# An attention-plus-MLP kernel's boot: two products moved to GpSimd, small state copies to ScalarE, and fewer filler matmuls

## The chip, the cores and the metric

The kernel runs on one core of a Trainium2 chip. A core has five engines with queues of their own: TensorE (PE, with its weight loads as PEld), VectorE (DVE), ScalarE (ACT), GpSimd (POOL) and SyncE (SP, which here only issues DMAs). Each engine works through its instructions in order and waits on semaphores for the others. The metric is the device time of one execution in microseconds, as the median of several runs; the kernel before takes 544.73 us (three runs, 544.55 to 544.80).

## The reference: what is computed

A linear attention with a decaying state, whose output feeds a layer pair with an unusual activation. For each batch (4), head (8) and token (768), with head dimension 48:

```
y_t   = r_t (state + (u * k_t) v_t^T)
state = diag(w_t) state + k_t v_t^T
```

The outputs, as x of 3072 tokens by 384, go through h = x w_in (384 by 2048), g = h - tanh(h), and out = g w_out (2048 by 384). All is float32.

## The kernel before, in words

The 3072 tokens are cut into eight blocks of 384 (four batches, two halves of the sequence each). For each block the attention is computed in chunks of 64 tokens; its result, transposed, lies in three tiles xT0 to xT2, and the layer pair takes it in 16 steps f: `first` (L869) multiplies w_in by xT into PSUM, three products per f, and the second product follows some steps later. While the layer pair of one block runs, the attention of the next is prepared by operations that `plan` (L1053) puts at given steps f. The order of PE, DVE, ACT and SP is written out by hand: what stands first in the program is issued first. POOL's order is the program's too. Waits are added by the framework from the tiles that are read and written. The first layer product of step f is followed by some no-operation instructions on PE (`SPACED`, L80: three behind each product in the first steps of block 0), and in block 0 each second-layer product by one.

Before block 0 can begin, `boot` (L1128) does the attention of block 0 with nothing beside it. It works in two halves of four heads each: h1 (pairs 2 and 3) and h2 (pairs 0 and 1), `HALVES`. For a half it does the following.

- `behind` (L420): a scan from the right over the decays w on DVE, into `post`; `take_whole` (L447) takes the whole chunk's decay from it.
- `times_behind` (L439): post becomes k times the scan, 128x768 on DVE.
- `times_u` (L451): ACT scales k by u in place, two instructions.
- `before` (L413): a reciprocal and a scan from the left into `pre` on DVE. `times_before` (L433): pre becomes r times that scan, on DVE.
- `own` (L507) and `earlier` (L510): the products of each chunk, r with k and pre with post, on PE; what they return is the masked copy into the score tile A on DVE (L502). `gram` (L474) does the products, and can put filler matmuls ahead of them: `passed` (L308, tiny 16x16 ones; the argument spare, 94 in h1) and `busy` (L301).
- `turn_1`, `turn_2` (L513, L521): PE transposes post, ACT copies the result to ks. `totals_by_column` (L620): ACT lays out the decays for the scan over states.
- `update_half` (L602): PE multiplies ks with v into two PSUM tiles, hp and acc (`by_column`), for the half's two pairs. `states_half` (L626): DVE scans over them, one scan a pair, into `first_states`, and returns two small adds (L632) which form the state that goes to block 1.
- `result("from_states")`, `result("from_scores")`: PE multiplies first_states by pre and v by A into PSUM; with apart=True the first goes pair by pair (`from_states`, L663), without it the pairs take turns within each chunk. `result_out` (L720) copies to xT and to the tile `late`; ACT does one half and, for h2, DVE the other.
- `fill_holes` (L773): six small DMAs of `late` into rows of xT that the copies leave free, in turn from SP and POOL.

Weights come as raw 64-bit pieces by DMA from SP (`more_weights`, `load_weights` L248) into five buffers and are converted by ACT (three instructions) and DVE (one), `convert` (L253). `begin_behind` holds a load until a given matmul is done: here until the state products of h1, the own products of h2 and the earlier products of h2.

Of the kernel before, what the change touches and what calls it, by code (L numbers as in the profile page):

```python
# [46 lines left out]
ALU = mybir.AluOpType  # L47
# [3 lines left out]
B, H, S, D = 4, 8, 768, 48  # L51
P = 128
L = 64
NB = 384
NQ = S // NB
NCH = NB // L
# [5 lines left out]
UP = 2  # L62
HALVES = (UP, 0)
ALL = tuple(range(NPAIR))
# [3 lines left out]
KC = DM // P  # L68
# [10 lines left out]
LATE = 3  # L79
SPACED = (3, 0), (0, 3), (3, 2), (2, 3), (3, 2), (2, 3), (3, 0), (0, 0)  # L80

# [45 lines left out]
def kernel(  # L127
# [12 lines left out]
    nc = tc.nc  # L140
# [179 lines left out]
    class Block:  # L320
# [111 lines left out]

        def times_before(self, p0, n):  # L433

            t = self.before_each(p0, n)
            return nc.vector.tensor_tensor(out=t, in0=self.tokens("r", p0, n).rearrange("d (c t) -> d c t", t=L),
                                           in1=t, op=ALU.mult)

        def times_behind(self, p0, n):  # L439


            t = self.half("post", p0, n * NCH * LP + 2)[:, 2:].rearrange("d (c j) -> d c j", j=LP)[:, :, 0:L]
            return nc.vector.tensor_tensor(
                out=self.half("post", p0, n * NB).rearrange("d (c t) -> d c t", t=L),
                in0=self.tokens("k", p0, n).rearrange("d (c t) -> d c t", t=L), in1=t, op=ALU.mult)
# [61 lines left out]
        def own(self, ps, p0, **fill):  # L507
            return self.masked(ps, "k", "r", masks["diagonal"], p0, **fill)

        def earlier(self, ps, p0, **fill):  # L510
            return self.masked(ps, "post", "pre", masks["above"], p0, **fill)
# [114 lines left out]
        def states_half(self, p0):  # L626

            for p in reversed(range(UP)):
                to, by, kv = (t.rearrange("d e c -> d (e c)") for t in
                              (first_states[:, p0 + p], first_totals[:, p0 + p], self.by_column[p]))  # L630
                nc.vector.tensor_tensor_scan(out=to, data0=kv, data1=by, initial=0.0, op0=ALU.add, op1=ALU.mult)
            return [lambda p=p0 + p, kv=kv: nc.vector.tensor_tensor(  # L632
                out=states[1][:, p, 0, 0:D], in0=first_states[:, p, :, NCH - 1], in1=kv[:, :, 0], op=ALU.add)
                for p, kv in enumerate(self.by_column)]

# [96 lines left out]
        def together(self, ps):  # L732
# [34 lines left out]
            for of in (from_state, scores) if self.q else (scores, from_state):  # L767
                for cross in range(2):
                    stretch(of, cross)
            self.result_out(ALL)  # L770
            self.fill_holes([nc.sync])

        def fill_holes(self, engines, which=range(2 * KC)):  # L773
            for n in reversed(which):
                i, h = n // 2, n % 2
                src = 64 * (n // KC) + 16 * (n % KC)
                engines[n % len(engines)].dma_start(out=self.xT[i][64 * h + D:64 * h + 64],
                                                    in_=self.late[src:src + 16, :])

# [273 lines left out]
    def plan(i):  # L1053
# [3 lines left out]
        if i == 0:  # L1057
            phases = {6: ("turn",), 7: ("update",), 10: ("earlier",), 13: ("results",)}
            before = {0: ("behind 2", "take_whole 2"), 2: ("behind 0", "take_whole 0"), 3: ("times_behind 2",),
                      4: ("times_behind 0",), 5: ("before 2",), 6: ("before 0",), 7: ("times_before",),  # L1060
# [51 lines left out]
    def run(ops):  # L1112
        for op in ops:
            op()
# [13 lines left out]
    def boot(ps, pair, blk, later):  # L1128
# [11 lines left out]
        blk.behind(h1, 1)  # L1140
        blk.take_whole(h1, UP)
        blk.totals_by_column(h1)
        nc.scalar.copy(out=later_ident, in_=ident)
        blk.before(h1, UP)
        blk.times_behind(h1, UP)
        blk.times_u(h1, UP)
        own = blk.own(ps, h1, spare=94, ahead=5, late=6)
        blk.turn_1(ps, h1)
        blk.times_before(h1, UP)
        earlier = blk.earlier(ps, h1)  # L1150
        blk.behind(h2, UP)
        blk.take_whole(h2, UP)
        first_a, first_b = convert(*raws.pop(0), tiles=2)
        own()
# [3 lines left out]
        begin_behind(blk.done, more_weights(nc.sync))  # L1158
        blk.times_behind(h2, UP)
        blk.times_u(h2, UP)  # L1160
        blk.turn_1(ps, h2)
        blk.turn_2(h2)
        earlier()
        blk.results(ps)
        blk.result("from_scores", both[0])
        run(blk.states_half(h1))
        blk.result("from_states", both[0], True, apart=True)
        blk.before(h2, UP)
        blk.update_half(pair, h2)
        blk.times_before(h2, UP)  # L1170
        own = blk.own(ps, h2)
# [5 lines left out]
        scored = blk.done  # L1177
        onwards = blk.states_half(h2)
        own()
        run(first_a[1:])  # L1180
        needed = 2 * KC - 2
        blk.fill_holes([nc.sync, nc.gpsimd], range(needed, 2 * KC))
        begin_behind(own_scored, more_weights(nc.sync))
        blk.fill_holes([nc.sync, nc.gpsimd], range(needed))
        begin_behind(scored, more_weights(nc.sync))
# [6 lines left out]
        blk.yp.reverse()  # L1192
        blk.result("from_states", both[1], apart=True)
        earlier(1, 1)
# [4 lines left out]
        more_weights(nc.sync)  # L1199
        run(onwards)  # L1200
        run(first_b[:1])
# [251 lines left out]
```

## Time and profile before

| | us |
|---|---|
| median of three runs | 544.73 |
| the profiled execution | 545.07 |
| its span in the profile | 543.3 |
| PE busy in the span | 534.1 |
| DVE busy | 459.0 |
| ACT busy | 403.7 |
| POOL busy | 6.5 |
| end of the boot: first layer product (L871) begins | 23.50 |

A row of a timeline reads: start in the span, length, engine, line, operation, the tile written and the tile read with their sizes, and the count of merged instructions; in brackets the idle time before it and what ended that. The lengths of merged rows run from the first start to the last end, and neighbours overlap a little since engines are pipelined; the distance of two starts is the better price of an instruction. In the costliest groups a row has count, busy time, mean ns, and then the idle time before them. A matmul of float32 shows as two passes, so a layer step is six rows of PE.

### The profile page before, as it was taken

How to read it: one execution, taken by the hardware profiler on the slowest of the kernel's cores; microseconds unless marked ns; L12 is line 12 of the kernel's file. 1: busy time of each engine (PE TensorE's matmuls, PEld its weight loads, DVE VectorE, ACT ScalarE, POOL GpSimd, SP SyncE). 2: the span in 40 equal slices, each digit the busy share in tenths (PEclk: the TensorE clock that was granted, in tenths of full speed). 3: DMA queues.
4: the chain of work that ended last, by engine and by line, in shares of the span. 5: the costliest groups of instructions: out<-in, count | busy, mean ns of one | idle time of the engine just before them, and what ended most of it. 6: DMA issues, size and time to landing. Idle time of an engine off the chain costs nothing.

```text
span 543.3 us, 14866 instructions
## 1 busy us (share of the span) xinstructions
PE 534.1 (98%) x5682; PEld 403.3 (74%) x5682; DVE 459.0 (84%) x943; ACT 403.7 (74%) x814; POOL 6.5 (1%) x47
## 2 busy tenths in 40 slices
PE   7999999999999999999999999999999999999996
PEld 5756665678877777777887787877788788777874
DVE  7999999999989989798997979879797997557463
ACT  4899986888668876688767886688866885766561
POOL 1100000000000000000000000000000000000000
PEclk9999999999999999999999999999999999999999
DMA  7798732252311631154112532136321420100101
GB/s 276 234 402 311 259 119 74 97 137 63 122 42 54 162 118 57 43 147 119 60 56 87 122 103 70 48 97 151 84 89 46 122 27 3 56 1 0 45 1 46
DMA packets 53048, 56.34 MB, mean 104 GB/s; under 512 B 21488, under 2 KB 50928, under 8 KB 52976
## 3 DMA queue, kind: packets, MB, share of 16 engines
q1 hardware_dynamic: 52592, 55.18, 33.9%
q8 instruction: 48, 0.79, 0.6%
q14 instruction: 24, 0.20, 0.1%
q10 hardware_dynamic: 288, 0.10, 0.1%
q0 software_dynamic: 96, 0.07, 0.1%
HBM read 44.73 MB, written 4.72 MB: 91 GB/s over the span
## 4 chain that ended last, share of the span: by engine, by line
PE 88%; DVE 6%; ACT 2%; issue 2%; DMA 1%; SPq 0%; DVEq 0%
PE hp L871 41%; PE acc L999 27%; PE att L999 7%; PE att L757 4%; PE acc L950 3%; PE acc L977 2%; PE att L494 2%; PE att L575 1%; PE att L871 1%; ACT up L264 1%; DMA r<-in_rT 1%; DVE w_sb L268 1%; PE acc L871 1%; DVE scores L502 1%; DVE states L587 1%
## 5 line engine op out<-in xcount | busy, mean ns | idle before, releaser
L871 PE MATMUL hp<-xT,w_sb 128*128 128x384 f32 x738 | 259.3, 488 | 0.4 <-ACT h L876 0.4
L871 PEld LDWEIGHTS hp<-xT,w_sb 128*128 128x128 f32 x738 | 131.8, 190 | 70.0 <-ACT h L876 1.3
L999 PE MATMUL acc<-forms,g 128*128 128x128 f32 x954 | 133.2, 276 | 0.0
L876 ACT ACTIVATE h<-hp 128x384 f32<-128x384 f32 x123 | 60.3, 490 | 96.6 <-PE hp L871 96.5
L999 PEld LDWEIGHTS acc<-forms,g 128*128 128x128 f32 x954 | 122.0, 192 | 10.3
L879 DVE SCALAR_TENSOR_TENSOR h<-h,s 128x384 f32<-128x384 f32 x128 | 70.5, 551 | 51.9 <-ACT s L894 51.8
L920 DVE TENSOR_TENSOR g<-g 128x256 f32<-128x256 f32 x265 | 103.2, 418 | 7.4 <-PE acc L999 6.5
L895 ACT ACTIVATE qa<-s,shift 128x384 f32<-128x384 f32 x113 | 69.5, 615 | 3.7
L897 ACT ACTIVATE junk<-s,shift 128x384 bf16<-128x384 f32 x113 | 67.7, 599 | 0.0
L879 DVE SCALAR_TENSOR_TENSOR g<-qa,h 128x384 f32<-128x384 f32 x112 | 61.6, 550 | 1.6 <-ACT qa L905 0.2
L894 ACT ACTIVATE s<-h 128x384 f32<-128x384 f32 x113 | 59.2, 523 | 3.6
L999 PEld LDWEIGHTS acc<-w_sb,g 128*128 128x128 f32 x318 | 46.8, 191 | 9.7 <-ACT sums L967 0.3
L999 PE MATMUL acc<-w_sb,g 128*128 128x128 f32 x318 | 53.0, 276 | 0.0
L999 PE MATMUL att<-w_sb,g 128*128 128x128 f32 x212 | 35.5, 275 | 0.0
L999 PEld LDWEIGHTS att<-w_sb,g 128*128 128x128 f32 x212 | 31.1, 192 | 5.3
L1034 DVE TENSOR_TENSOR sums<-sums 128x256 f32<-128x256 f32 x84 | 32.8, 406 | 1.7 <-ACT sums L1011 1.4
L950 PE MATMUL acc<-w_sb,sums 128*128 128x384 f32 x96 | 33.9, 489 | 0.1
L264 ACT ACTIVATE up<-raw 128x768 f16<-128x768 f32 (+1 forms) x32 | 33.1, 1074 | 0.0
L950 PEld LDWEIGHTS acc<-w_sb,sums 128*128 128x128 f32 x96 | 17.9, 190 | 13.0 <-DVE sums L879 1.2
L417 DVE TENSOR_TENSOR_SCAN pre<-w,start 128x780 f32<-128x780 f32 x14 | 25.0, 1783 | 0.8
L429 DVE TENSOR_TENSOR_SCAN post<-w,seed 128x780 f32<-128x780 f32 x14 | 24.9, 1775 | 0.0
L897 ACT ACTIVATION_READ_ACCUMULATOR junk<-s,shift 128x1 f32 x113 | 21.1, 187 | 0.0
(118 smaller groups left out, 528.8 us busy)
## 6 DMA issues: line engine op xcount, KB each, us to landing
raw<-in_weights SPq DMA_DIRECT2D x16, 768.0 KB, 7.1
w<-in_wT SPq DMA_DIRECT2D x7, 780.0 KB, 4.7
k<-in_kT SPq DMA_DIRECT2D x7, 768.0 KB, 4.6
r<-in_rT SPq DMA_DIRECT2D x7, 768.0 KB, 4.6
v_sb<-in_v SPq DMA_DIRECT2D x8, 576.0 KB, 4.0
k<-in_tokens SPq DMA_DIRECT2D x7, 576.0 KB, 5.0
r<-in_tokens SPq DMA_DIRECT2D x7, 576.0 KB, 4.7
out_y<-sums SPq DMA_DIRECT2D x18, 128.0 KB, 1.8
```

The lines of the kernel that those rows point to most:

```text
L264: return lambda: nc.scalar.activation(out=to, in_=of, func=AF.Copy, scale=scale, bias=bias)
L417: return nc.vector.tensor_tensor_scan(out=self.tile("pre")[:, cols], data0=self.tile("w")[:, cols], data1=start[:, 0:n * NCH * LP], initia ...
L871: nc.tensor.matmul(hp, lhsT=w_in_sb[:, f, kc, :], rhs=xT[kc], start=(kc == KC - 1), stop=(kc == 0))
L876: return h, nc.scalar.activation(out=h, in_=hp, func=AF.Copy, scale=1.0 / UPSCALE)
L879: return lambda: nc.vector.scalar_tensor_tensor(out=out, in0=in0, scalar=scalar, in1=in1, op0=op0, op1=ALU.mult)
L894: nc.scalar.activation(out=s, in_=h, func=AF.Square)
L895: nc.scalar.activation(out=qa, in_=s, func=AF.Square, bias=shift[:, 4:5])
L897: nc.scalar.activation(out=junk[:, 0:NB], in_=s, func=AF.Relu, bias=shift[:, 5:6], accum_out=excess[:, at:at + 1])
L920: return lambda: nc.vector.tensor_tensor(out=G[:, to:to + 2], in0=two(G, g_at(q, a0), g_at(q, a1)), in1=two(G, g_at(q, b0), g_at(q, b1)), ...
L950: nc.tensor.matmul(acc, lhsT=g[:, j * P:(j + 1) * P], rhs=w_out_sb[:, f, :], start=(f == self.first), stop=(f == NF - 1))
L999: nc.tensor.matmul(to, lhsT=G[:, g_at(q, a), :], rhs=rhs, start=start, stop=stop, skip_group_check=True)
L1034: ops.append(lambda op=op, at=at: nc.vector.tensor_tensor(out=at[0], in0=at[1], in1=at[2], op=OPS[op]))
```

## The change

In `boot`: `times_behind` of h1 is issued before `totals_by_column` and `before`. `times_behind` and `times_before` of h2 are issued on POOL instead of DVE, the first right behind `take_whole`, the second behind `before` of h2. The four small adds that finish the state (L632) are split: ACT copies the last term of the sum from PSUM (`last_half`, two copies of 128x48 a half), and one add of 128x192 (`onwards`) follows in step 3 of block 0. For h1 the two copies stand between ACT's scaling by u for h2 and its copy to ks; for h2 between the first and the second weight piece. The masked copy of own products of h2 now comes before the scans over states of h2 on DVE. The products from states of h2 no longer go pair by pair. Four of the fills of holes go out on SP, and xT0's two on POOL. The tiny filler pairs are 38 instead of 94, and the no-operations behind the first layer's products of block 0 are six instead of three. In the kernel's general path, which this input does not take, result_out gets other copies.

```diff
@@ -77,7 +77,8 @@
 UNITS = [(0, 0), (0, 1)] + [u for j in range(NF // 2 - 2) for u in ((1, j), (0, j + 2))] + [(1, NF // 2 - 2),
                                                                                       (1, NF // 2 - 1)]
 LATE = 3
-SPACED = (3, 0), (0, 3), (3, 2), (2, 3), (3, 2), (2, 3), (3, 0), (0, 0)
+SPARE = 38
+SPACED = (6, 0), (0, 3), (3, 2), (2, 3), (3, 2), (2, 3), (3, 0), (0, 0)
 
 
 
@@ -430,17 +431,17 @@
                 out=back(t[:, 0:width]), data0=back(self.tile("w")[:, a:a + width]),
                 data1=back(seed[:, 0:width]), initial=1.0, op0=ALU.mult, op1=ALU.max)
 
-        def times_before(self, p0, n):
+        def times_before(self, p0, n, engine=nc.vector):
 
             t = self.before_each(p0, n)
-            return nc.vector.tensor_tensor(out=t, in0=self.tokens("r", p0, n).rearrange("d (c t) -> d c t", t=L),
+            return engine.tensor_tensor(out=t, in0=self.tokens("r", p0, n).rearrange("d (c t) -> d c t", t=L),
                                            in1=t, op=ALU.mult)
 
-        def times_behind(self, p0, n):
+        def times_behind(self, p0, n, engine=nc.vector):
 
 
             t = self.half("post", p0, n * NCH * LP + 2)[:, 2:].rearrange("d (c j) -> d c j", j=LP)[:, :, 0:L]
-            return nc.vector.tensor_tensor(
+            return engine.tensor_tensor(
                 out=self.half("post", p0, n * NB).rearrange("d (c t) -> d c t", t=L),
                 in0=self.tokens("k", p0, n).rearrange("d (c t) -> d c t", t=L), in1=t, op=ALU.mult)
 
@@ -629,9 +630,15 @@
                 to, by, kv = (t.rearrange("d e c -> d (e c)") for t in
                               (first_states[:, p0 + p], first_totals[:, p0 + p], self.by_column[p]))
                 nc.vector.tensor_tensor_scan(out=to, data0=kv, data1=by, initial=0.0, op0=ALU.add, op1=ALU.mult)
-            return [lambda p=p0 + p, kv=kv: nc.vector.tensor_tensor(
-                out=states[1][:, p, 0, 0:D], in0=first_states[:, p, :, NCH - 1], in1=kv[:, :, 0], op=ALU.add)
-                for p, kv in enumerate(self.by_column)]
+
+        def last_half(self, p0):
+
+            for p, kv in enumerate(self.by_column):
+                nc.scalar.copy(out=states[1][:, p0 + p, 0, 0:D], in_=kv[:, :, 0])
+
+        def onwards(self, p0, n):
+            to = states[1][:, p0:p0 + n, 0, 0:D]
+            nc.vector.tensor_tensor(out=to, in0=first_states[:, p0:p0 + n, :, NCH - 1], in1=to, op=ALU.add)
 
         def update_any(self, ps, p0, tot):
             ks, last = self.ks[:, p0:p0 + UP], self.q == NQ - 1
@@ -767,15 +774,14 @@
             for of in (from_state, scores) if self.q else (scores, from_state):
                 for cross in range(2):
                     stretch(of, cross)
-            self.result_out(ALL)
-            self.fill_holes([nc.sync])
-
-        def fill_holes(self, engines, which=range(2 * KC)):
+            self.result_out(ALL, None if spread else [nc.scalar.copy] * 2)
+            self.fill_holes()
+
+        def fill_holes(self, which=range(2 * KC), engine=nc.sync):
             for n in reversed(which):
                 i, h = n // 2, n % 2
                 src = 64 * (n // KC) + 16 * (n % KC)
-                engines[n % len(engines)].dma_start(out=self.xT[i][64 * h + D:64 * h + 64],
-                                                    in_=self.late[src:src + 16, :])
+                engine.dma_start(out=self.xT[i][64 * h + D:64 * h + 64], in_=self.late[src:src + 16, :])
 
         def phase(self, ps, name):
 
@@ -1056,7 +1062,7 @@
         formed_w = {}
         if i == 0:
             phases = {6: ("turn",), 7: ("update",), 10: ("earlier",), 13: ("results",)}
-            before = {0: ("behind 2", "take_whole 2"), 2: ("behind 0", "take_whole 0"), 3: ("times_behind 2",),
+            before = {0: ("behind 2", "take_whole 2"), 2: ("behind 0", "take_whole 0"), 3: ("times_behind 2", "onwards"),
                       4: ("times_behind 0",), 5: ("before 2",), 6: ("before 0",), 7: ("times_before",),
                       9: ("product_u", "held", "bound 2"), 10: ("product_r", "bound 0"), 11: ("product_sum",), 12: ("diagonal_in 2", "diagonal_in 0")}
             ahead = {}
@@ -1139,35 +1145,36 @@
         blk.behind(h1 + 1, 1)
         blk.behind(h1, 1)
         blk.take_whole(h1, UP)
+        blk.times_behind(h1, UP)
         blk.totals_by_column(h1)
         nc.scalar.copy(out=later_ident, in_=ident)
         blk.before(h1, UP)
-        blk.times_behind(h1, UP)
         blk.times_u(h1, UP)
-        own = blk.own(ps, h1, spare=94, ahead=5, late=6)
+        own = blk.own(ps, h1, spare=SPARE, ahead=5, late=6)
         blk.turn_1(ps, h1)
         blk.times_before(h1, UP)
         earlier = blk.earlier(ps, h1)
         blk.behind(h2, UP)
         blk.take_whole(h2, UP)
+        blk.times_behind(h2, UP, nc.gpsimd)
         first_a, first_b = convert(*raws.pop(0), tiles=2)
         own()
         blk.turn_2(h1)
         blk.totals_by_column(h2)
         blk.update_half(pair, h1)
         begin_behind(blk.done, more_weights(nc.sync))
-        blk.times_behind(h2, UP)
         blk.times_u(h2, UP)
         blk.turn_1(ps, h2)
+        earlier()
+        blk.last_half(h1)
         blk.turn_2(h2)
-        earlier()
         blk.results(ps)
         blk.result("from_scores", both[0])
-        run(blk.states_half(h1))
+        blk.states_half(h1)
         blk.result("from_states", both[0], True, apart=True)
         blk.before(h2, UP)
+        blk.times_before(h2, UP, nc.gpsimd)
         blk.update_half(pair, h2)
-        blk.times_before(h2, UP)
         own = blk.own(ps, h2)
         own_scored = blk.done
         run(first_a[:1])
@@ -1175,13 +1182,14 @@
         blk.result_out((2,))
         earlier = blk.earlier(ps, h2, ahead=1)
         scored = blk.done
-        onwards = blk.states_half(h2)
         own()
+        blk.states_half(h2)
         run(first_a[1:])
-        needed = 2 * KC - 2
-        blk.fill_holes([nc.sync, nc.gpsimd], range(needed, 2 * KC))
+        blk.last_half(h2)
+        blk.fill_holes(range(4, 6))
         begin_behind(own_scored, more_weights(nc.sync))
-        blk.fill_holes([nc.sync, nc.gpsimd], range(needed))
+        blk.fill_holes(range(2, 4))
+        blk.fill_holes(range(2), nc.gpsimd)
         begin_behind(scored, more_weights(nc.sync))
         later.load("w")
         second_a, second_b = convert(*raws.pop(0))
@@ -1190,14 +1198,13 @@
         more_weights(nc.sync)
         blk.results(ps)
         blk.yp.reverse()
-        blk.result("from_states", both[1], apart=True)
+        blk.result("from_states", both[1])
         earlier(1, 1)
         earlier(0, 1)
         for p in reversed(both[1]):
             blk.result("from_scores", (p,), True, more=True)
         later.load("k")
         more_weights(nc.sync)
-        run(onwards)
         run(first_b[:1])
         for p in reversed(both[1]):
             blk.result_out((p,), [nc.scalar.copy, nc.vector.tensor_copy])
```

## The prediction

> **What bounds the kernel now.** I read the page first (shares, then the chain of work that ended last), then TensorE's timeline, then those of the other engines in the first 50 us.
>
> ```profile
> span 543.3 us, 14866 instructions
> PE 534.1 (98%) x5682; PEld 403.3 (74%) x5682; DVE 459.0 (84%) x943; ACT 403.7 (74%) x814; POOL 6.5 (1%) x47
> ...
> PEclk9999999999999999999999999999999999999999
> ...
> PE 88%; DVE 6%; ACT 2%; issue 2%; DMA 1%; SPq 0%; DVEq 0%
> ```
>
> TensorE (PE) is busy for 98% and holds 88% of the chain. So a microsecond that the boot gains or loses moves the end by a microsecond, except where PE waits once more later and so can catch up. Only the boot is edited, with two small edits in block 0. PE's timeline around the seam (start, length):
>
> ```profile
> 13.38 0.87 PE L517 MATMUL att<-ident,post 128*128 128x128 f32 x6
> 18.00 0.90 PE L494 MATMUL att<-r,k 48*64 48x64 f32 x48
> 20.06 2.38 PE L679 MATMUL att<-pre,first_states 48*48 48x64 f32 x46
> ...
> 23.50 4.56 PE L871 MATMUL acc<-xT,w_sb 128*128 128x384 f32 x12
> 27.89 2.10 PE L871 MATMUL hp<-xT,w_sb 128*128 128x384 f32 x6
> 29.83 2.10 PE L871 MATMUL att<-xT,w_sb 128*128 128x384 f32 x6
> ...
> 44.85 2.10 PE L950 MATMUL acc<-w_sb,sums 128*128 128x384 f32 x6
> 47.33 2.20 PE L871 MATMUL hp<-xT,w_sb 128*128 128x384 f32 x6 [0.38 <-ACT h L876]
> ```
>
> From the second half's transposes (13.38) to the first product of the layer (23.50) PE hardly pauses. Afterwards a group of six takes 1.94 us (27.89 to 29.83) back to back; the last real wait is the one at 47.33 (44.85 + 1.94 = 46.79, so 0.54 lost). The boot's PE order is the same in both kernels, so its other engines decide. ScalarE (ACT):
>
> ```profile
> 13.36 1.12 ACT L454 ACTIVATE k<-k,u_sb 128x384 f32<-128x384 f32 x2 [0.80 <-DVE post L443]
> 14.38 0.78 ACT L523 COPY ks<-att 128x768 f32<-128x768 f32 x1
> 19.86 0.89 ACT L264 ACTIVATE w_sb<-raw 128x768 f32<-128x768 f32 x1
> 20.66 1.96 ACT L264 ACTIVATE up<-raw 128x768 f16<-128x768 f32 x2
> 23.29 0.84 ACT L729 COPY xT<-att 48x384 f32<-48x384 f32 x2 [0.67 <-PE att L697]
> ...
> 36.59 0.92 ACT L264 ACTIVATE w_sb<-raw 128x768 f32<-128x768 f32 x1 [0.85 <-DMA raw<-in_weights]
> ```
>
> and VectorE (DVE):
>
> ```profile
> 12.36 0.96 DVE L443 TENSOR_TENSOR post<-k,post 128x768 f32<-128x768 f32 x1
> 13.24 1.02 DVE L502 COPY_PREDICATED scores<-mask_all,att 128x768 f32<-128x768 uint8 x1
> 14.15 0.74 DVE L631 TENSOR_TENSOR_SCAN first_states<-acc,first_totals 128x288 f32<-128x288 f32 x1
> ...
> 15.57 0.24 DVE L632 TENSOR_TENSOR states<-first_states,hp 128x48 f32<-128x48 f32 x1
> 15.88 0.22 DVE L416 RECIPROCAL start<-whole 128x12 f32<-128x12 f32 x1
> 16.14 1.78 DVE L417 TENSOR_TENSOR_SCAN pre<-states,start 128x780 f32<-128x780 f32 x1
> 17.95 0.96 DVE L436 TENSOR_TENSOR pre<-r,pre 128x768 f32<-128x768 f32 x1
> 19.50 0.73 DVE L631 TENSOR_TENSOR_SCAN first_states<-hp,first_totals 128x288 f32<-128x288 f32 x1
> 20.14 2.20 DVE L502 COPY_PREDICATED scores<-mask_all,att 128x768 f32<-128x768 uint8 x3
> 23.80 1.04 DVE L729 COPY xT<-att 48x384 f32<-48x384 f32 x2 [0.74 <-ACT xT L729]
> ```
>
> DVE has no gap from 14.15 to 22.34. The last row matters: DVE waited 0.74 us for ACT although both only read the same PSUM tile. Two engines that read one PSUM tile are put in program order. The change lets ACT read the two PSUM tiles of the state products (hp and acc) which DVE's scans read, so the same kind of wait arises there. The built program of the changed kernel confirms it: the first half's scans wait for ACT's two new copies, and in the second half ACT's two copies wait for DVE's scans.
>
> **The change part by part.** First the two products on GpSimd (POOL), which DVE did at 12.36 and 17.95.
>
> ```profile
> 3.88 0.68 SPq L369 DMA_DIRECT2D k<-in_kT  x1
> k<-in_kT SPq DMA_DIRECT2D x1, 384.0 KB, 8.4
> L245 POOL MEMSET ones<- 128x1 f32 x1 | 0.1, 88 | 0.0
> masks.py:199 POOL TENSOR_SCALAR_AFFINE_SELECT ident<-ident 128x128 f32<-128x128 f32 x1 | 0.3, 283 | 0.0
> ```
>
> The second half's k lands at 3.88 + 8.4 = 12.28, just before DVE multiplied it, so POOL cannot start earlier than DVE did. The trace has no product on POOL. The nearest row has one float input: 283 ns for 128 elements, of which 88 are there for a single element, leaves 1.5 ns an element, so 768 elements take about 1.2 us; a second input read one after the other would make that 2.3. From below, DVE's own 0.96 bounds it. I take the middle of the last two, 1.75, as an estimate, and 0.1 to begin: done at 14.15 instead of 13.32, **0.83 late**. [...]
>
> What waits for it: ACT's scaling of k by u (L454) writes k in place and so begins at 14.18 instead of 13.36. Behind it in ACT's order now stand the first half's two copies (128x48), then the copy to ks. The two scalings hold ACT for 1.02 (13.36 to 14.38), so the copies begin at 15.20; two of them at some 0.2 each (an estimate: ks, with 768 elements, takes 0.78) end at 15.55. DVE's first-half scans, which wait for them, begin at 15.6 instead of 14.15: **1.45 late**, with DVE idle meanwhile. Two adds less (15.57 to 15.88) return 0.31: the scan for "pre" starts at 15.6 + 1.99 - 0.31 = 17.28 and ends at 19.06. POOL's second product then runs from 19.15 to 20.9, where DVE was through at 18.91: 2.0 late for the second half's "earlier" products.
>
> PE: transposes at 14.2; from there to the end of the own-chunk products (L494) it is 18.90 - 13.38 = 5.52 as before, so 19.72 (before 18.90). Now DVE's order counts: the change puts that mask ahead of the second half's scans. Mask 19.75 to 20.7 (0.91 from 13.24 to 14.15), two scans 1.4 (14.15 to 15.57): they end at 22.1 instead of 20.23. PE's products from states, which now need both scans, then run from 22.15. They are no longer split by pair, so that four quadrants of the array take turns:
>
> ```profile
> 78.24 1.56 PE L757 MATMUL att<-pre,states 48*48 48x64 f32 x96
> 24.41 0.30 PEld L871 LDWEIGHTS acc<-xT,w_sb 128*128 128x128 f32 x2 [0.62 <-DVE xT L729]
> ```
>
> Interleaved, 96 take 1.56, so 48 take about 0.8 instead of 2.38. That gain of 1.5 is real, and PE is done with the boot's products at 24.05, only 0.5 late. But ACT reads the second half's state sums behind the scans: 22.15 to 22.5. It has stood idle for these since about 20.3. Behind them in its queue are a weight conversion of three (19.86 to 22.62, 2.76; 2.65 by starts) and only then the copies of the attention's result to xT. These begin at 25.15 instead of 23.29; DVE's halves wait for ACT's (25.65 instead of 23.80), and PE, which began on xT1 at 24.41 when DVE had copied it, begins at 26.25. **The layer starts 1.85 late.**
>
> Of that, later slack returns some: 0.54 at 47.33, and about 0.15 in shorter steps of 0.1, so 0.7 of PE's waits shrink. ACT itself waited 0.85 for weights at 36.59. Of their loads on SP, one stands behind a fill of holes more than before, and two are gated by the ends of the own and of the "earlier" products (0.8 and about 1.8 late, since these now begin at 20.95 and were over by 20.1), so I put the weights some 1.2 late, which agrees. **Sum: +1.85 - 0.7 = +1.15 us.**
>
> The rest costs nothing, each with its cover:
>
> ```profile
> 2.08 2.50 PE L312 MATMUL att<-ident 128*16 128x16 bf16 x94 [2.08 <-POOL ident masks.py:199]
> 6.48 0.30 PEld L305 LDWEIGHTS <-later_ident 128*128 128x128 bf16 x2 [0.55 <-ACT later_ident L1143]
> 5.74 0.23 DVE L416 RECIPROCAL start<-whole 128x12 f32<-128x12 f32 x1
> 1.86 0.43 SPq L369 DMA_DIRECT2D k<-in_kT  x1
> k<-in_kT SPq DMA_DIRECT2D x1, 384.0 KB, 4.4
> DVE sums L879 <- ACT qa L905: 1.4, 5, 0.4
> ```
>
> 56 pairs fewer end PE's filler 56 x 26 ns = 1.5 us sooner, but the next filler waits for ACT until 6.48 in any case. The first half's product now stands ahead of "pre" on DVE, where it waits for k (1.86 + 4.4 = 6.26) while DVE was ready at 5.74: 0.5 late, which ends in the idle time before 15.6, 1.45 long and longer by the product that left (0.88, 12.36 to 13.24); without that cover it would cost the 0.5. The four small adds (0.31 a pair) become one in block 0, of at most 0.6, inside DVE's five waits for ACT of 1.4 together. Behind POOL's second product stand two fills of xT0; at 20.9 PE needs them only five us later. The nops: a group with nine keeps the pace of 1.94, so a nop lasts at most 0.21 us; eighteen stay hidden in a group if one lasts under 0.107.
>
> The profiled execution took 545.07 us (span 543.3 and 1.8 around it), 0.34 above the median of 544.73. The sum gives 546.2 for such an execution and 545.9 for a median. With POOL at 0.96 instead of 1.75 everything comes 0.8 earlier (+0.35); at 2.3, 0.55 later (+1.7).
>
> **The rivals.**
>
> *PE alone sets the boot's end: faster.* PE never paused between 13.38 and 23.50, and the products from states shed 1.5. If POOL is about as quick as DVE, and ACT's and DVE's reads of hp and acc do not hold each other, the layer starts 0.6 to 1.5 sooner: 543.7. For it: the unbroken PE rows. Against it: DVE's row at 23.80 shows exactly such a hold. It decides in favour of faster once the second scans end before 20.3, that is, if the own products end before 17.9.
>
> *The weights hide it: no change.* ACT waited 0.85 us for loads. If the loads come no later than before, and PE finds more slack than the 0.7, at most about 0.4 remains: 545.1. Against it: the loads' gates move too.
>
> *The nops, or the clock: clearly slower.* In block 0 a first-layer group with eighteen nops is paired with a second-layer group with three. At 0.2 us a nop these 21 take 4.2 against 3.87, 0.33 on each of 14 pairs, 4.6: 550.5. Likewise PE now waits about 2 us around 24 to 26, and no row shows how its clock takes that. The Trainium skill, TensorE: Matmul & The Clock Gate, section "Part 1: The HAM clock gate (the 'warmup' mystery)", says that an idle window of about 3.4 us halves PE's clock. By it, two groups at half pace would cost 3.9 us more, 549.8; the granted clock of the trace (the row PEclk) is at 9 tenths or more in every slice, but no gap behind the boot's begin is as long.
>
> **How the numbers follow.** Forecast (a slower start, 0.3 to 2 us net): 0.62, of which about 0.38 lies over 0.2% (1.09 us, about what a measurement of this kernel can tell from no change) and 0.24 within it. PE alone: 0.20, of which 0.15 passes 0.2% and 0.05 does not. Weights hide it: 0.09, within. Nops or clock: 0.09, slower. So slower 0.47, same 0.38, faster 0.15. The likeliest time is 545.9, in its own range 545.0 to 546.7. Part of both outer cases must be inside, so 543.9 to 547.2.
>
> **What would show each step.** POOL's products as rows of about 1.75 us from 12.4 and 19.2. On ACT, the copies of states from 15.2, and a gap of over 1 us before the second pair. On DVE, a gap before the first scans released by "ACT states", and the own mask ahead of the second scans. On PE, from-states products of under 1 us, and the wait for xT1 until about 26.2. Wrong would be: first scans near 14.2, no gap on ACT near 21, groups of the layer at another pace than 1.94, or a POOL product far from 1.75.

## The result, and the profile after

| | before | after |
|---|---|---|
| median, us | 544.64 (544.31 to 544.80, 4 runs) | 549.05 (548.94 to 549.36, 4 runs) |
| ratio, 95% interval | | 1.0083 (1.0065 to 1.0100) |
| profiled execution, span | 545.07, 543.3 | 548.94, 547.1 |
| TensorE: first step f=2 of the layer (hp) begins | 27.89 | 31.59 |

The kernel is 4.4 us slower; 545.9 was forecast, and 547.2 was the upper end of the range. The page after: span, busy time, the queue of the engines' own code, and the chain's shares.

```profile
span 547.1 us, 14879 instructions
PE 534.2 (98%) x5626; PEld 403.0 (74%) x5626; DVE 457.1 (84%) x938; ACT 404.0 (74%) x818; POOL 9.4 (2%) x48
...
q8 instruction: 48, 0.79, 0.7%
...
PE 91%; DVE 5%; issue 1%; DMA 1%; PEld 1%; POOL 0%; PEldq 0%; SPq 0%; DVEq 0%; POOLq 0%
```

TensorE's busy time is the same in sum (534.1 before, 534.2 after), so the time lost is, net, waiting. Within that sum the shorter filler (1.11 us instead of 2.50) and the interleaved from_states (1.34 instead of 2.38) are made up by rows that ran slower (own of h1 1.56 instead of 1.08, from_scores of h2 1.53 instead of 0.89). TensorE's timeline of the boot (start, length, in brackets the idle time before a row and what ended it):

```profile
14.38 0.88 PE L518 MATMUL att<-ident,post 128*128 128x128 f32 x6 [0.47 <-POOL post L444]
15.18 0.44 PE L704 MATMUL att<-scores,v_sb 64*48 64x64 f32 x16
15.93 0.68 PE L704 MATMUL att<-scores,v_sb 64*48 64x64 f32 x32 [0.30 <-issue]
...
19.39 0.30 PE L495 MATMUL att<-r,k 48*64 48x64 f32 x6
20.52 0.91 PE L495 MATMUL att<-r,k 48*64 48x64 f32 x42 [0.83 <-issue]
...
23.91 1.34 PE L686 MATMUL att<-pre,first_states 48*48 48x64 f32 x48 [1.30 <-DVE first_states L632]
25.52 1.53 PE L704 MATMUL att<-scores,v_sb 64*48 64x64 f32 x48 [0.27 <-PEq L724]
26.98 4.77 PE L877 MATMUL acc<-xT,w_sb 128*128 128x384 f32 x12
31.59 2.10 PE L877 MATMUL hp<-xT,w_sb 128*128 128x384 f32 x6
33.53 0.81 PE L877 MATMUL att<-xT,w_sb 128*128 128x384 f32 x2
```

Two groups are cut in the middle, by 0.30 and 0.83 us of "issue": TensorE waits for nothing that the profile shows. Nothing of the kind was in the boot before. GpSimd's timeline after:

```profile
12.64 1.68 POOL L444 TENSOR_TENSOR post<-k,post 128x768 f32<-128x768 f32 x1 [9.44 <-DVE whole L450]
19.11 1.67 POOL L437 TENSOR_TENSOR pre<-r,pre 128x768 f32<-128x768 f32 x1 [4.79 <-DVE pre L418]
```

ScalarE's:

```profile
15.38 0.18 ACT L637 COPY states<-hp 128x48 f32<-128x48 f32 x1
...
23.95 0.20 ACT L637 COPY states<-hp 128x48 f32<-128x48 f32 x1 [2.59 <-DVE first_states L632]
...
26.82 0.82 ACT L736 COPY xT<-att 48x384 f32<-48x384 f32 x2
```

and VectorE's:

```profile
15.69 0.76 DVE L632 TENSOR_TENSOR_SCAN first_states<-acc,first_totals 128x288 f32<-128x288 f32 x1 [1.15 <-ACT states L637]
...
17.25 1.78 DVE L418 TENSOR_TENSOR_SCAN pre<-states,start 128x780 f32<-128x780 f32 x1
...
21.54 1.04 DVE L503 COPY_PREDICATED scores<-mask_all,att 128x768 f32<-128x768 uint8 x1 [2.51 <-PE att L495]
...
27.30 1.04 DVE L736 COPY xT<-att 48x384 f32<-48x384 f32 x2 [2.04 <-ACT xT L736]
```

Up to 17.25 the forecast's row times hold within 0.2 us. From the own products of h2 on everything is late. Last, TensorE after by stretches of 1 us (busy share, instructions, granted clock as PEclk, DMA share, GB/s):

```profile
24.00:25.00 1.00, 1.00 (x48) 0.95 0.97 389
25.00:26.00 1.00, 0.73 (x30) 0.50 0.91 169
26.00:27.00 1.00, 1.00 (x41) 0.50 0.82 270
27.00:28.00 1.00, 1.00 (x6) 0.50 0.91 369
28.00:29.00 1.00, 1.00 (x3) 0.85 0.98 347
```

The clock is halved for 3.4 us: (0.05 + 3 x 0.50 + 0.15) / 0.5. The page's row of 40 slices did not show it.

Where the 3.70 us at f=2 comes from: the own products of h2 end at 21.43 instead of 18.90 (+2.53 against +0.82 forecast), and from there to f=2 it is 10.16 instead of 8.99 (+1.17; forecast +1.03). Later, waits give back and take again: the lag is 2.81 at 52.7 and 3.34 from 81 to TensorE's last product.

### The profile page after: what moved, and what is told of

It reads as the page before. It is cut to its first block, busy times and chain, and to the rows that moved or that the text cites. A ratio compares the mean times of both kernels' runs of the same rounds, so it can differ in the third digit from the quotient of the medians.

```text
span 547.1 us, 14879 instructions
## 1 busy us (share of the span) xinstructions
PE 534.2 (98%) x5626; PEld 403.0 (74%) x5626; DVE 457.1 (84%) x938; ACT 404.0 (74%) x818; POOL 9.4 (2%) x48
## 4 chain that ended last, share of the span: by engine, by line
PE 91%; DVE 5%; issue 1%; DMA 1%; PEld 1%; POOL 0%; PEldq 0%; SPq 0%; DVEq 0%; POOLq 0%
PE hp L877 42%; PE acc L1005 26%; PE att L1005 6%; PE acc L956 4%; PE att L764 4%; PE att L495 2%; PE acc L983 2%; PE att L576 2%; PE att L877 1%; DMA k<-in_kT 1%; PE acc L877 1%; DVE states L588 1%; DVE w_sb L269 1%; DVE sums L885 0%; PEld att L686 0%
```

## The experiments

Four theories were set against each other. **Ring** (called B): the waits through GpSimd, ScalarE and VectorE make all of the loss. **Code** (A): the stops on "issue" are TensorE waiting for its own instructions, whose place in memory the 56 pairs shift. **Order and clock** (D): the new order leaves TensorE idle, and the clock drops behind that. **Holes** came up on the way: the last fills of xT land too late.

The code theory rests on counting. The queue "instruction" moved 0.79 MB in 48 packets, 16.4 KB each; the program of after has 12,267 instructions on TensorE (two weight loads and two passes for a float32 product, one for a no-operation), so about 256 in a packet. e1, with 12,379 instructions, moved 49 packets, which fits. By this count the stops in after stand near 474 and 730 instructions into the program, 256 apart; such places, 256 instructions apart, are called marks below. The change takes 112 out of the boot and puts 126 no-operations into block 0, so from there on the code stands as before but for 15 instructions.

**e1, after with 94 pairs; e2, before with 38; e5, before with 38 and the six no-operations.**

```diff
-SPARE = 38                                             # e1
+SPARE = 94
-        own = blk.own(ps, h1, spare=94, ahead=5, late=6)   # e2, e5
+        own = blk.own(ps, h1, spare=38, ahead=5, late=6)
-SPACED = (3, 0), (0, 3), (3, 2), (2, 3), (3, 2), (2, 3), (3, 0), (0, 0)   # e5
+SPACED = (6, 0), (0, 3), (3, 2), (2, 3), (3, 2), (2, 3), (3, 0), (0, 0)
```

> The kernel after, with the 56 tiny matmul pairs put back (94 again). Theory A (TensorE's code comes late): in the profile after, TensorE stops twice on 'issue', with no semaphore behind it, after 16 matmuls of from_scores of the first half (0.30 us idle) and after 6 of own of the second half (0.83 us), 256 instructions apart by count (four to an f32 product); with 112 instructions more ahead of them the stops go, own of the second half ends near 19.6 us and not at 21.4, and the time falls by 1.3 to 2 us, to 547.0 to 547.7 us. Theory B (the ring of waits through ScalarE's copies and GpSimd makes all of it): the two stops stay and the time stays at 549.0, within 0.3 us.

> The kernel before with 38 tiny pairs instead of 94 and nothing else. Theory A: the stops on 'issue' show up in the kernel before too, in from_scores of the first half (until about 15.9 us) and in own of the second half (until about 20.5 us, where it runs at 18.0 to 18.9 us now), and the time rises by 0.8 to 1.8 us, to 545.5 to 546.5 us. Theory B: the pairs fill idle time only; 544.6 us, within 0.3 us.

> The kernel before with 38 tiny pairs and, in block 0, 6 empty instructions behind each matmul of the first product instead of 3, as in the change; nothing else. In e2 (38 pairs alone) the first layer's f=2 came 3.59 us later, and six stops on 'issue' of 0.92 to 3.05 us followed in together, each at the same place of the code modulo 256 instructions; there the code stood 112 instructions ahead of where it stands before, here it stands 14 behind. Theory A (code): the six stops go, the boot's 3.6 us stays, of which later waits give back about 1: 547.0 to 548.2 us. Theory B (the pairs only fill idle time, the ring makes the loss): 544.6 us, within 0.3 us.

Measured: e1 561.35 us (ratio to before 1.0317, 1.0294 to 1.0340), e2 559.02 (1.0248, 1.0220 to 1.0276), e5 546.91 (1.0035, 1.0016 to 1.0054). The size of e1 and e2 was far off both theories, and the place tells why. The view of waits of e1 has a new row for TensorE (us in total, times, longest):

```profile
PE att L764 <- issue: 7.3, 6, 2.4
```

The first of these six in e1's timeline:

```profile
86.40 1.09 PE L764 MATMUL att<-scores,v_sb 64*48 64x64 f32 x26 [2.40 <-issue]
```

and the first of six in e2's:

```profile
86.83 1.30 PE L757 MATMUL att<-scores,v_sb 64*48 64x64 f32 x35 [3.05 <-issue]
```

In `together` 384 or 352 small instructions follow each other. Counted through the program, the twelve stops of e1 and e2 stand at 241 or 242 modulo 256, though the two codes differ by 239 instructions. (The stops in the boot stand at 218 to 220 by the same count; why the two places differ stays open.) Each is at the second such mark within one run of small products. The one run of seven that is left, the second in time, whose first mark stands within its first 18 instructions, has no stop, and neither have before, after and e5, with one mark in each run. e5 puts the code of `together` back and keeps the boot's: the six stops go, and its timeline has these three, at the marks near 474, 730 and 986:

```profile
15.88 0.68 PE L697 MATMUL att<-scores,v_sb 64*48 64x64 f32 x32 [1.26 <-issue]
20.59 0.91 PE L494 MATMUL att<-r,k 48*64 48x64 f32 x42 [0.95 <-issue]
24.62 0.72 PE L679 MATMUL att<-pre,first_states 48*48 48x64 f32 x11 [0.60 <-issue]
```

The three sum to 2.81 us, and f=2 comes 2.74 us later than in before (30.64), at a full clock. The pairs and no-operations alone, without GpSimd or ScalarE, cost the kernel before 2.3 us, as A said (547.0), and B's "only fill idle time" falls. From one mark's stop to the next it took 4.0 to 4.7 us here, while TensorE gets through 256 small instructions in 2.1 (96 passes and their weight loads in 1.56).

A doesn't tell when a mark brings a stop. In e2, whose boot has the code of e5's, the stops near 474 and 730 did not come, only the one near 986 (0.60). Its f=2 is late by even more, 3.59 us, because TensorE's rows ran slow from about 10 to 18 us: six transposes of h2 took 1.54 us instead of 0.87. That is what they take in e18 at a clock of 0.50, but the granted clock of e2 reads 1.00 there. What made these rows slow isn't shown.

**e3, sums back on VectorE; e4, products back on VectorE** (both on after).

```diff
-        blk.last_half(h1)                              # e3; h2 and onwards likewise
-        blk.states_half(h1)
+        run(blk.states_half(h1))
-        blk.times_behind(h2, UP, nc.gpsimd)            # e4
+        blk.times_behind(h2, UP)
-        blk.times_before(h2, UP, nc.gpsimd)
+        blk.times_before(h2, UP)
```

> The kernel after with the states' last sums back on VectorE (no ScalarE copies, four small adds as in the kernel before, none in block 0); GpSimd's products and the 38 pairs stay. Theory A: VectorE's scans of the first half start near 14.6 us and not 15.7, but own of the second half still stops for TensorE's code until about 20.5 us, so the time stays within 0.6 us of 549.0. Theory B: what hangs on the ring goes, first-half scans to the first layer product come 1.1 us or more earlier, and the time falls to about 547.5 us.

> The kernel after with both products of the second half back on VectorE; ScalarE's copies and the 38 pairs stay. Theory A: the transposes of the second half start near 13.7 us, but from_scores still stops until about 15.9 us and own of the second half until about 20.5 us; the time stays within 0.6 us of 549.0. Theory B: GpSimd's slower products (1.68 us against 0.96 us) are in the ring, and the time falls by 0.7 to 1.5 us, to 547.5 to 548.3 us.

Measured: e3 548.20 (1.0068, 1.0044 to 1.0093), e4 549.07 (1.0074, 1.0052 to 1.0095). VectorE's scans of h1 do start at 14.18 in e3, 1.5 us sooner, and the own products of h2 still stop, until 20.02 in both. B would have had 1.5 us from e3; it got 0.85, between that and A's 0.6, with an interval that overlaps that of after. At f=2 only 0.34 us of it is there (31.25); some 0.4 comes later, from the small add of block 0, which e3 takes back too (see below). So at f=2 the stops cover most of the 1.5 us: the own products of h2 end at 20.93, not 21.43. e4 gains nothing, but it doesn't test the products alone: its first product stands ahead of VectorE's two masks, so that the transposes wait for these until 14.29, and its clock was halved for 6.8 us, not 3.4.

**e6, e7, e8: 94 pairs and 3 no-operations with the change's new order; e6 whole, e7 with sums, e8 with sums and products back on VectorE.** The edits are those of e1, e3 and e4, with SPACED as in before.

> The kernel after with 94 pairs and 3 empty instructions, as before the change: GpSimd's products, ScalarE's sums and the new order stay. Theory A: no stop on 'issue', neither in the boot nor in together; but e1's boot stays (transposes of the second half behind GpSimd's product near 14.07 us after an idle TensorE, clock 0.50 in 15 to 17 us, f=2 near 31.2 us): 547.5 to 548.6 us. Theory B: as after, 549.0 us, within 0.3 us.

> e6 with the states' sums back on VectorE too: left are GpSimd's products and the new order. Theory A: own of the second half ends near 19.7 to 20.2 us, f=2 near 30.3 to 31.0 us: 546.8 to 548.0 us. Theory B, whose ring is cut here: no later than 545.5 us.

> e7 with the products back on VectorE too: left is the new order alone (own mask ahead of the scans of the second half, from_states of the second half interleaved, the other holes' queues and copies). Theory A and B: transposes near 13.4 us, no idle TensorE and no drop of the clock, own of the second half ends near 18.9 us, f=2 at 28.0 to 29.2 us: 544.7 to 546.0 us. If it stays above 547, the order itself is a cause that neither theory has.

Measured: e6 549.98 (1.0092, 1.0065 to 1.0119), e7 548.24 (1.0068, 1.0038 to 1.0098), e8 550.31 (1.0095, 1.0073 to 1.0117). The stops ahead of the own products of h2 are gone (they end at 19.93 in e6, 19.65 in e7), as A said; one of 1.42 us came up behind them in e6. But the time isn't clearly lower (e7 gains 0.8 us, and the intervals overlap), and e8, which has neither GpSimd's products nor ScalarE's sums, is no faster than e6: here A fails as the whole story, and B with it. In e8 part is its own doing, since the product now stands ahead of VectorE's two masks and the transposes waited for these (14.30). Of the 3.84 us by which its f=2 is late (31.73), 1.10 is there at the end of the own products of h2 (20.00), and 1.65 more comes in at the head of the layer, where the clock is halved: 0.50 from about 23 to 29 us, 6.8 us long, twice that of after. The first twelve passes of the layer, 4.56 us before, in e8's timeline:

```profile
25.69 6.21 PE L880 MATMUL acc<-xT,w_sb 128*128 128x384 f32 x12
```

The runs of one kernel follow it: the four of e7 took 546.98 us at a mean clock of 0.997, 548.05 and 548.43 at 0.992, 550.85 at 0.983.

**e9, scans ahead of the own mask; e10, four idle matmuls ahead of from_states** (both on after); **e11, the new order in before.**

```diff
-        own()                                          # e9; e11 the other way round,
-        blk.states_half(h2)                            # and without apart=True
+        blk.states_half(h2)
+        own()
+        busy(blk.yp[0][:, 0], 4)                       # e10
         blk.result("from_states", both[1])
```

> The kernel after with VectorE's two state scans of the second half ahead of its own mask again, as in the kernel before; nothing else. Theory D (the new order leaves TensorE idle behind it and the clock drops): in after, TensorE waits 1.30 us for the scans ahead of from_states of the second half, and the granted clock is 0.50 from 25 to 28 us; with the scans at 19.5 to 20.9 us (their products end near 19.4) the wait goes, the first layer product starts 0.9 to 1.5 us earlier at a full or shorter-lowered clock: 546.8 to 548.0 us. Theory A (code alone: own of the second half still stops until 20.5 us) without D: within 0.5 us of 549.0.

> The kernel after with four idle 512-column bf16 matmuls on TensorE ahead of from_states of the second half, where it sits idle for 1.30 us (about 0.31 us each, from the six of 1.89 us in the kernel before). They compute nothing that is used. Theory D's second half (the idle stretch lowers the clock, which then costs the layer): the granted clock stays at or near 1.00 in 24 to 29 us, from_scores takes 0.9 us instead of 1.53, and the time falls by 0.3 to 1.2 us. If the clock costs nothing because the copies bind there: 549.0 us, within 0.3 us; if they delay from_states: up to 0.3 us more.

> The kernel before with the new order of the second half alone: VectorE's own mask ahead of its two state scans, and from_states of the second half in one interleaved run behind both. Products, sums, pairs and empty instructions as before. Theory D: from_states of the second half starts near 21.4 us instead of 20.0 and TensorE idles for about 1.2 us ahead of it; from_scores about 0.2 us later at a full clock (544.7 to 545.2 us), and where the clock drops to 0.50 behind the idle stretch, 1.5 to 3 us more (546.0 to 548.0). Theories A and B: 544.6 us, within 0.3 us.

Measured: e9 548.22 (1.0064, 1.0040 to 1.0088), e10 548.37 (1.0059, 1.0039 to 1.0080), e11 545.05 (0.9996, 0.9978 to 1.0014). e10 keeps the clock: all four runs at 0.999 or more (after: 0.992 to 0.997), and two of the stretches above read in e10

```profile
25.00:26.00 1.00, 0.74 (x47) 1.00 0.92 168
26.00:27.00 1.00, 1.00 (x30) 1.00 0.76 283
```

So in this kernel the idle matmuls do prevent the drop. It is worth 0.3 us at f=2 (31.30) and 0.7 in the medians, whose intervals overlap. In e9 the wait for the scans is gone (from_states at 22.08) and f=2 comes 1.27 sooner, within D's 0.9 to 1.5, though TensorE stops for 0.57 and 0.55 and waits 0.78 for a DMA ahead of it. The median gains 0.8, and D's upper end of 548.0 is just missed; two of the four runs had a mean clock of 0.994 and 0.985. e11 shows both halves of D in its profile, a late from_states (21.53) and a clock of 0.50, and a stop of 0.73 on "issue" besides. Its f=2 is 1.59 late, of which later waits gave back 0.8. The medians show no difference, with an interval that reaches to 0.8 us.

**e12, before with from_states interleaved and two sums moved; e16, before with eight idle matmuls ahead of own of h1.**

```diff
-        run(onwards)                                   # e12, and without apart=True
         run(first_b[:1])
+        run(onwards)
-        own = blk.own(ps, h1, spare=94, ahead=5, late=6)   # e16
+        own = blk.own(ps, h1, spare=94, ahead=5, late=8)
```

> The kernel before with from_states of the second half interleaved (1.3 to 1.6 us instead of 2.38) and the two last sums of VectorE moved behind its next weight piece; the rest as before. from_scores of the second half waits for these sums now (0.24 us): it and the first layer product come 0.2 to 0.3 us earlier, 544.3 to 544.5 us; if what TensorE saves there turns into idle time and the clock drops, 545 to 547 us.

> The kernel before with eight instead of six idle matmuls on later_ident, in the 0.82 us that TensorE waits for k at 8.5 to 9.3 us. If the runs of the kernel before at a mean clock of 0.995 or less (546 to 547.7 us) come from that idle stretch: all runs at 0.998 or more and a median of 544.3 to 544.5; if not, 544.6 within 0.3 us.

Measured: e12 544.89 (0.9999, 0.9989 to 1.0009), e16 545.12 (1.0006, 0.9988 to 1.0024): neither is faster. In e16 the spread of before stays (544.15 to 548.07, the two slowest at a clock of 0.993), so that idle stretch isn't its cause.

**e13, e14, e15: code moved to 74 pairs and 4 no-operations; e17, e18: code of before, old order, idle matmuls ahead of the transposes.** They were to show the ring alone.

```diff
+SPARE = 74                                             # e13 to e15
+SPACED = (4, 0), (0, 3), (3, 2), (2, 3), (3, 2), (2, 3), (3, 0), (0, 0)
+            busy(tp[:, 0], ahead)      # in turn_1 of h2, ahead=3: all but e14
+        busy(blk.yp[0][:, 0], 4)                       # e13, e14
+        blk.states_half(h2)            # ahead of own(): e15, e17, e18
```

> The kernel after with 74 pairs and 4 empty instructions (the code in together stands within 2 instructions of e6's place, and in the boot the 256-instruction marks fall just inside own of the first half and 2 records before the end of earlier of the second half), and idle bf16 matmuls where TensorE waits: three ahead of the second half's transposes, four ahead of its from_states. If the ring costs what the forecast gave it and the rest of the loss is code and clock: clock at 0.997 or more, no stop on 'issue' over 0.6 us, f=2 at 29.6 to 30.4 us, 545.8 to 547.2 us. If the ring itself costs more than the forecast said: 548 us or more at a full clock.

> e11 (the kernel before with the new order of own mask, scans and from_states) with 74 pairs, 4 empty instructions and four idle matmuls ahead of from_states of the second half. Without the ring, with code and clock held: 544.3 to 545.2 us; the difference to e13 is what the ring costs, 1.0 to 2.0 us. If the order costs by itself: 545.5 us or more at a full clock.

> e13 with the scans ahead of the own mask as in the kernel before, and without the four idle matmuls ahead of from_states (no wait should be left there). 545.3 to 546.6 us, 0.3 to 0.8 below e13, if the order costs beside the ring; equal to e13 within 0.3 if not.

> The kernel after with 94 pairs and 3 empty instructions, VectorE's scans of the second half ahead of the own mask as in the kernel before, and three idle bf16 matmuls ahead of the second half's transposes. The forecast's ring (h1 scans 1.15 us late behind ScalarE's copies, own of the second half 0.9 to 1.1 us late): f=2 at 29.2 to 30.0 us and 545.6 to 546.6 us, if code and clock are held; a stop on 'issue' in earlier of the second half, as in e6 (1.42 us), would add up to that: to 548. At or above 548.5 with a full clock and no such stop: the ring costs more than the forecast said.

> e17 with the states' sums on VectorE as in the kernel before: GpSimd's products alone. h1 scans near 14.2 us (e7: 14.10), own of the second half ends near 19.6 to 20.0 us, f=2 at 28.5 to 29.5 us, 544.9 to 545.9 us with the clock held, 0.4 to 1.0 below e17 if the sums are the larger part of the ring; equal to e17 within 0.3 us if GpSimd's product alone sets it.

Measured: e13 549.51 (1.0073, 1.0049 to 1.0097), e14 548.69 (1.0083, 1.0056 to 1.0109), e15 550.96 (1.0115, 1.0084 to 1.0147), e17 549.27 (1.0075, 1.0049 to 1.0100), e18 548.60 (1.0062, 1.0042 to 1.0082). All miss. In e13 to e15 the mark 474 fell into update of h1, and TensorE stopped there for 2.34, 2.48 and 1.21 us; e14 has no ring at all and loses 3.8 us. e17 and e18 did hold the code (no stop), but e18 not the clock, which was 0.50 between 14 and 16 us. e17 meets the forecast's times within 0.3 us: own products of h2 end at 20.01, the boot's products at 24.16 (forecast 24.05, for the new order of mask and scans; e17 has the old one). Then, in its timeline:

```profile
24.09 0.91 PE L878 MATMUL acc<-xT,w_sb 128*128 128x384 f32 x2
27.28 5.16 PE L878 MATMUL acc<-xT,w_sb 128*128 128x384 f32 x10 [2.28 <-DMA xT<-late]
```

The layer waits 2.28 us for a fill of xT's holes, and the clock drops behind that. The two passes ahead of the wait take the last part of xT, and the ten behind it begin with xT1. SyncE issues the fills of xT1 (in before it shares them with GpSimd), behind a piece of the weights that goes out when the own products of h2 have ended. SyncE's timeline in before:

```profile
18.95 0.41 SPq L251 DMA_DIRECT2D raw<-in_weights  x1
19.42 1.15 SPq L777 DMA_DIRECT2D xT<-late  x2
```

and in e17:

```profile
20.53 0.52 SPq L252 DMA_DIRECT2D raw<-in_weights  x1
21.10 1.14 SPq L785 DMA_DIRECT2D xT<-late  x2
```

The view of DMAs from 14 to 33 us has the median time from issue to landing last; before:

```profile
xT<-late SPq DMA_DIRECT2D x3, 24.0 KB, 4.5
```

and e17:

```profile
xT<-late SPq DMA_DIRECT2D x4, 24.0 KB, 3.7
xT<-late POOLq DMA_DIRECT2D x2, 24.0 KB, 5.7
```

The 3.7 is a median over two fills ahead of the weights, which took about 2.0 us, and two behind them, which took 5.5 to 5.7. In before the fills behind the weights landed at 23.9 and 25.1, just in time; in e17 they go out 1.7 us later, and TensorE waits for them until 27.28. GpSimd's own fills, which follow its second product, are of the part of xT that is used last. They aren't what binds: in e13, e15 and e18 they landed in 1.7 to 2.8 us, and TensorE still waited 1.38, 2.15 and 1.57 for those of SyncE. e9 waits too (0.78), and so does e16 (0.94), which has before's fills and no product on GpSimd. In after no row waits for them, the layer being later still. What the ring costs by itself stays open: no run removed stops, clock drop and late fills together. No version beats the kernel before.

## Why the prediction was wrong, point by point

**Right.** GpSimd's product: 1.75 forecast, 1.68 measured (0.83 late became 1.0, since it began 0.24 later, when VectorE was through with "whole"). Copies from 15.2: 15.38. Scans of h1 15.6: 15.69, released by "ACT states". "Pre" 17.28: 17.25. The own mask ahead of the scans, the 2.4 us from the own products' end to from_states (19.72 to 22.15; measured 21.43 to 23.91), ScalarE's gap of over 1 us near 21 (2.59), its copies to xT 5.4 us behind the own products (25.15; 26.82 from 21.43). The ring's rows and the direction came as forecast; the ring's own price in the kernel's time is not shown, since the stops cover part of it. The pace of 1.94 with six no-operations holds too (31.59 to 33.53), so the first half of the last rival falls.

**Failed: "56 pairs fewer ... the next filler waits for ACT until 6.48 in any case", at nothing.** The working looked at the time that the pairs fill and not at the place of what stands behind them. The step where it shows is "from there to the end of the own-chunk products it is 5.52 as before": 7.05 in after (14.38 to 21.43). Of the 1.71 us by which 19.72 was missed, 0.18 is the transposes' later start, 0.39 lies around the first stop, 1.14 in the own products with the second (2.04 instead of 0.90). e5 shows the stops in a kernel without any ring, where they and the pairs cost 2.3 us; e6, e7 and e17, which have none there, end the own products at 19.65 to 20.01. Why a mark brings a stop in one row and none in another stays open.

**Too low: from_states interleaved in 0.8 us.** It took 1.34 (1.26 or 1.27 in ten of the variants), against 2.38. ScalarE's conversions hid the error.

**Failed: the small add "inside DVE's waits".** In block 0 it stands in an unbroken row of VectorE's timeline:

```profile
42.69 0.95 DVE L444 TENSOR_TENSOR post<-k,post 128x768 f32<-128x768 f32 x1
43.56 0.49 DVE L641 TENSOR_TENSOR states<-first_states,states 128x192 f32<-128x192 f32 x1
43.97 0.95 DVE L269 SCALAR_TENSOR_TENSOR w_sb<-w_sb,up 128x768 int32<-128x768 int32 x1
```

and TensorE, which waited 0.26 at the same place before, now waits for VectorE's sums:

```profile
79.44 2.20 PE L956 MATMUL acc<-w_sb,sums 128*128 128x384 f32 x6 [0.63 <-DVE sums L885]
```

Between 52.7 and 81 us the lag behind before grows by 0.50 to 0.54 in after, e4, e6, e9, e10, e13 and e15 (0.39 in e17), which have the add, and by 0.10 to 0.12 in e3, e5, e7, e8, e11, e14, e16 and e18, which don't: about 0.42 us. With it the return of 0.7 became 0.36.

The sum at the end of TensorE's work: 1.15 forecast + 1.71 (own products of h2) + 0.14 (between them and f=2) + 0.34 (less given back) = 3.34, as measured. 0.5 more lies behind TensorE's last product (4.9 us before, 5.4 after), which makes the 3.87 us between the two profiled executions; the medians are 4.4 apart. Every kernel made from after has 5.4 to 5.5 us there and every one made from before 4.9 to 5.0, whichever sums, products, pairs or no-operations it puts back. The cause of these 0.5 us stays open.

**The rivals.** "The clock" came about, at a time near the one named, and was priced too high for this execution: 0.3 us at f=2, since ScalarE's copies bind there. Where they don't (e8) it is worth the 1.65 us by which the first twelve passes grew. The Trainium skill, "TensorE: Matmul & The Clock Gate", section "Part 1: The HAM clock gate (the 'warmup' mystery)", gives a free-running window of 3413 ns; the drops here last 3.4 us (after, e11, e17) or 6.8 (e4, e6, e7, e8), which agrees. "PE alone" and "weights hide it" found nothing for them.

## What to carry to other kernels

Instructions have a place as well as a duration: where an engine runs hundreds of small ones in a row, whatever shifts the code ahead of them (fillers, no-operations) moves the marks at which it can stop, and no count of microseconds shows it. Before an item is priced at nothing because it fills idle time, change it alone in the old kernel; e5 would have shown half of the loss. And in a boot where several chains end within a microsecond or two, taking one delay away brings out the next, so prices taken from single removals don't add up.

## What the runs showed of the hardware that was not expected

- TensorE can stop with no semaphore involved: 0.25 to 3.05 us, at places 256 instructions apart. From one stop's end to the next it took 3.7 to 4.9 us in the boots of after, e3, e5, e9 and e10. What sets that time stays open, and so does whether a mark brings a stop at all: the kernel before ran over the mark near 986 without one (a row of 1.03 us from 19.15), where e6 stopped for 1.42 and e11, with the boot code of before in another order, for 0.73.
- The halved clock comes in units of 3.4 us, and behind stretches in which TensorE was by no means idle: in e8 its busy share was 0.96, 0.54 and 0.51 in the three microseconds before.
- GpSimd's float32 product of 128x768 took 1.68 us, VectorE's 0.96: 1.75 times. The Trainium skill, "GPSIMD Engine Reference", section "Performance versus the Vector engine", gives 1.96 for an add of 2048 float32 elements; no run here has that size, and for the product of 768 the measurement decides.
